# Two chained expert layers: another form of the first layer's division, and another order of its products

## The chip, the cores and the metric

The kernel runs on one core of a Trainium2 chip. The metric is the device time of one execution in microseconds; less is better. Three timed runs of the kernel before gave 1129.43, 1130.37 and 1132.01 us, with the median 1130.37 us.

## The reference, cut to what matters

6080 tokens of width 256 pass a gated scan over time and then two layers with 2048 hidden columns each. All of it is float32.

```python
h = f[:, t] * h + i[:, t] * x[:, t]            # the scan, f = lb + (1 - lb) * sigmoid(f_logit)

h = x @ w_in                                   # stage 1
P = a[0] + a[1] * h + a[2] * h**2 + a[3] * h**3
Q = 1.0 + np.abs(b[0]) * np.abs(h) + np.abs(b[1]) * h**2
g = P / (Q + 1e-06)
x2 = g @ w_out

h = x2 @ w_in                                  # stage 2, with weights of its own
r = np.maximum(h, 0.0)
out = (r * r) @ w_out
```

## The kernel before, in words

Tokens are cut into 12 blocks, the first of 448 tokens and eleven of 512 (`BLOCKS`). The 2048 hidden columns of a stage are taken 256 at a time, so a block has `NP` = 8 **steps** for each stage. From the third loop on (line 727), one step of stage 1, `a`, runs beside one step of stage 2, `b`, which lies `LAG` = 9 steps behind. "Position" below is a step's number in its block of stage 1, 0 to 7. A matrix product is made of a high and a low part of both operands: three terms, each a pass of matmuls with 512 tokens, as `mm1` and `mm2` show. So one full step of the third loop has 12 matmuls of `S1_mm1` (tile `h`), 12 of `S2_mm1` (tile `hb`), 12 of `S1_mm2` (tile `acc`, inputs `g1h` and `g1l`) and 12 of `S2_mm2` (inputs `g2h` and `g2l`), of which the last four, `S2_mm2_low`, are held over to the next step.

The order on each engine is the order in which the program is written (`manual_schedule`); every engine takes its own instructions strictly in that order. Blocks 0 and 1 go through two loops of their own (lines 658 and 691), where part of the work still is in single float32 products; the third loop begins with block 2.

In a step of the third loop, stage 1 runs as follows. `s1_scalar` (line 402) reads the products `h` from PSUM: ScalarE writes `u` = |h| (L412) and `s` = a3 h + a2 (L420), GpSimd writes `t` = |b1| u + |b0| (L414). `s1_quad` (L432) on VectorE makes `t` = t u, which is Q without its constant. `s1_poly` (L424, L425) makes `s` the polynomial without a0. `s1_rsqrt` (L446, L447) makes `u` about 1/Q on ScalarE, as the square of a reciprocal root. `s1_ratio` (L461, L464) makes `t` = Q u and `s` = -P u; the sign comes from `pna`, which line 565 has negated. `s1_high` (L470) rounds -s to the high part `g1h` on ScalarE. `s1_low` (L475, L478) corrects the quotient, (t - 2) s, and leaves the low part `g1l`, both on VectorE. `g1h` and `g1l` have one buffer each; `u`, `t`, `s` and `r` have two; the PSUM tile `h` has one, so the next `S1_mm1` can start only when `s1_poly` has read it.

Stage 2 is `s2_relu` (L485) and `s2_square` (L491, L496) on ScalarE, and `s2_low` (L501), which makes `g2l` on GpSimd one step later. Ahead of it stands a copy of one element of `t` on GpSimd (L751): it makes `g2l` wait until `s1_quad` of the same step is done.

`ahead` (line 603) puts the preparation of the next block into certain positions: loads of `z` at 2 and of `x` at 3, the gate `pre_gate` at 3 (two transposes on VectorE, a tanh with a table load on ScalarE, two operations on GpSimd), transposes `pre_in` at 4, a multiplication and a scan at 5 and 6. `split_x` (L319, L320) follows at 7, `out_store` at 2. At position 0 of the next block `to_x2` (L509, L510) turns the finished sum `acc` into `x2h` and `x2l`, the input of stage 2. `z`, `x` and the output tile share one buffer.

The order of the products is set by lines 764 and 777:

```python
            if ap is not None and (ends or a is None or not bp[0]):
                S1_mm2(*ap)
            ...
            if ap is not None and not (ends or a is None or not bp[0]):
                S1_mm2(*ap)
```

In a full step `S1_mm2` so comes behind `S2_mm2_high`; where a block ends (`ends`, position 0), ahead of it.

Of the kernel before, what the change touches and what calls it, by code (L numbers as in the profile page):

```python
# [15 lines left out]
P = 128  # L16
# [8 lines left out]
def hgru_two_moe_kernel(  # L25
# [49 lines left out]
    def f32(ap):  # L75
        return ap.bitcast(F32)
# [184 lines left out]

    def pre_gate(j):
        n = BLOCKS[j]
        t = pt.pop(("z", j))
        for dc in range(KD):
            sg = pre.tile([P, NMAX], F32, tag="sg", name="sg")
            nc.vector.transpose(sg[:, :n], squares(t, j)[:, :, dc::KD])
            nc.scalar.activation(out=sg[:, :n], in_=sg[:, :n], func=ACTF.Tanh, scale=0.5)
# [4 lines left out]
            pt["f", j, dc] = sg  # L273

# [174 lines left out]
    def s1_single(a, h, u, t, s):  # L449
# [4 lines left out]
        nc.vector.scalar_tensor_tensor(  # L454
            out=g, in0=t, scalar=2.0, in1=s, op0=ALU.subtract, op1=ALU.mult
        )
# [10 lines left out]

    def s1_high(a, s):
        fh = chain_tile("g1h", F32R, BLOCKS[a[0]])
        nc.scalar.activation(out=fh, in_=s, func=ACTF.Copy, scale=-1.0)  # L470
        return fh

    def s1_low(a, t, s, fh, eng):
        fl = chain_tile("g1l", F32R, BLOCKS[a[0]])
        nc.vector.scalar_tensor_tensor(  # L475
            out=t, in0=t, scalar=2.0, in1=s, op0=ALU.subtract, op1=ALU.mult
        )
        eng.tensor_tensor(out=fl, in0=t, in1=f32(fh), op=ALU.subtract)  # L478
        g1[a] = (fh, fl)
# [23 lines left out]

    def to_x2(j):
        n = BLOCKS[j]
        a = acc.pop((1, j))
        h = io.tile([P, KD, NMAX], F32R, tag="x2h", name="x2h")
        l = io.tile([P, KD, NMAX], F32R, tag="x2l", name="x2l")
        nc.scalar.activation(out=h[:, :, :n], in_=a[:, :, :n], func=ACTF.Copy)  # L509
        nc.vector.tensor_tensor(  # L510
# [31 lines left out]
    with tc.manual_schedule():  # L542
# [115 lines left out]
        for i in range(NP):  # L658
# [32 lines left out]
        for s in range(NP, 2 * NP):  # L691
# [35 lines left out]
        for s in range(2 * NP, n1 + LAG + 1):  # L727
# [8 lines left out]
            if a is not None:  # L736
# [32 lines left out]
            if bp is not None and not last_hand_over:  # L769
# [52 lines left out]
```

## Time and profile before

| what | us |
|---|---|
| median of three runs | 1130.37 |
| the profiled execution | 1131.16 |
| its span in the trace | 1129.2 |
| TensorE busy with matmuls | 1106.3 (98%) |
| VectorE busy | 984.2 (87%) |
| ScalarE busy | 886.9 (79%) |
| GpSimd busy | 439.5 (39%) |

The profiled execution's own time is 1131.16 us, 2.0 us above its span, and 0.8 us above the median. PE is TensorE's matmuls, PEld its weight loads, DVE is VectorE, ACT is ScalarE, POOL is GpSimd, SP issues most transfers. A row of the timeline has the start in the span, the length, the engine, the line and the tiles (out<-in), and in brackets how long the engine was idle before and who ended that. Two instructions of one engine overlap a little in such rows, so what an instruction costs its engine is read from start to start. A row of the windows view has the stretch, its length, and for each engine the busy time and in brackets the instructions. Matmul lengths in the rows are modelled; starts are what to go by.

### The profile page before, as it was taken

How to read it: one execution, taken by the hardware profiler on the slowest of the kernel's cores; microseconds unless marked ns; L12 is line 12 of the kernel's file. 1: busy time of each engine (PE TensorE's matmuls, PEld its weight loads, DVE VectorE, ACT ScalarE, POOL GpSimd, SP SyncE). 2: the span in 40 equal slices, each digit the busy share in tenths (PEclk: the TensorE clock that was granted, in tenths of full speed). 3: DMA queues.
4: the chain of work that ended last, by engine and by line, in shares of the span. 5: the costliest groups of instructions: out<-in, count | busy, mean ns of one | idle time of the engine just before them, and what ended most of it. 6: DMA issues, size and time to landing. Idle time of an engine off the chain costs nothing.

```text
span 1129.2 us, 12488 instructions
## 1 busy us (share of the span) xinstructions
PE 1106.3 (98%) x4594; PEld 860.4 (76%) x4594; DVE 984.2 (87%) x885; ACT 886.9 (79%) x993; POOL 439.5 (39%) x308
## 2 busy tenths in 40 slices
PE   8999999999999999999999999999999999999997
PEld 5446666777887887887888788788788788788876
DVE  6998998889989989989989989989998998998732
ACT  5866987987787887887787787788788788787754
POOL 3536542344343353444343343444334344433200
PEclk9999999999999999999999999999999999999999
DMA  9943322320200200110020030030021021010010
GB/s 248 338 124 70 73 45 49 73 37 1 38 19 1 38 20 1 19 38 1 5 53 1 1 57 1 1 57 1 1 38 19 1 38 19 0 20 1 1 19 19
DMA packets 107164, 44.65 MB, mean 40 GB/s; under 512 B 95840, under 2 KB 96736, under 8 KB 107104
## 3 DMA queue, kind: packets, MB, share of 16 engines
q1 hardware_dynamic: 103136, 35.21, 13.9%
q0 software_dynamic: 2448, 8.39, 4.0%
q8 instruction: 36, 0.59, 0.2%
q10 hardware_dynamic: 1520, 0.27, 0.1%
q14 instruction: 24, 0.20, 0.1%
HBM read 29.23 MB, written 6.23 MB: 31 GB/s over the span
## 4 chain that ended last, share of the span: by engine, by line
PE 43%; DVE 25%; issue 6%; ACT 3%; POOL 1%; DVEq 0%; ACTq 0%
PE acc L346 21%; PE hb L332 12%; PE h L332 11%; DVE s L424 4%; DVE s L425 4%; DVE s L464 3%; DVE t L432 3%; DVE g1l L478 3%; DVE t L461 2%; DVE t L475 2%; POOL t L414 1%; DVE sg L299 1%; DVE x1l L320 1%; ACT g1h L470 1%; DVE x2l L510 1%
## 5 line engine op out<-in xcount | busy, mean ns | idle before, releaser
L414 POOL TENSOR_SCALAR t<-u,pb 128x1024 f32<-128x1024 f32 x88 | 136.1, 1547 | 358.6 <-ACT u L412 358.6
L332 PE MATMUL hb<-x2h,wi 128*128 128x512 f32 (+1 forms) x768 | 203.9, 387 | 0.0
L501 POOL TENSOR_TENSOR g2l<-r,g2h 128x1024 fp32r<-128x1024 f32 x78 | 188.4, 2416 | 8.4 <-PE acc L346 8.2
L346 PE MATMUL acc<-g2h,wo 128*128 128x512 f32 x704 | 174.9, 390 | 1.1 <-ACT g2h L496 0.7
L332 PEld LDWEIGHTS hb<-x2h,wi 128*128 128x128 f32 x768 | 144.2, 188 | 29.0
L346 PEld LDWEIGHTS acc<-g2h,wo 128*128 128x128 f32 x704 | 132.2, 188 | 30.1 <-ACT g2h L496 2.0
L432 DVE TENSOR_TENSOR t<-t,u 128x1024 f32<-128x1024 f32 x88 | 107.0, 1216 | 50.3 <-POOL t L414 50.3
L485 ACT ACTIVATE r<-hb 128x512 f32<-128x512 f32 (+1 forms) x192 | 109.4, 593 | 50.8 <-PE hb L332 47.9
L446 ACT ACTIVATE u<-t 128x1024 f32<-128x1024 f32 x88 | 93.4, 1061 | 65.5 <-DVE t L432 65.1
L478 DVE TENSOR_TENSOR g1l<-t,g1h 128x1024 fp32r<-128x1024 f32 x80 | 126.2, 1578 | 18.0 <-ACT g1h L470 9.2
L461 DVE SCALAR_TENSOR_TENSOR t<-t,u 128x1024 f32<-128x1024 f32 x88 | 121.8, 1385 | 9.9 <-ACT u L447 7.9
L470 ACT ACTIVATE g1h<-s 128x1024 fp32r<-128x1024 f32 x80 | 84.8, 1060 | 52.7 <-DVE s L464 52.7
L425 DVE SCALAR_TENSOR_TENSOR s<-s,pna,h 128x1024 f32<-128x1024 f32 (+1 forms) x96 | 121.9, 1270 | 3.4
L464 DVE SCALAR_TENSOR_TENSOR s<-s,pna,u 128x1024 f32<-128x1024 f32 (+1 forms) x96 | 121.3, 1264 | 0.0
L332 PE MATMUL h<-x1h,wc 128*128 128x512 f32 x352 | 115.7, 410 | 5.3 <-DVE s L425 5.3
L332 PE MATMUL hb<-x2l,wi 128*128 128x512 f32 (+1 forms) x384 | 117.5, 387 | 0.0
L424 DVE TENSOR_TENSOR s<-s,h 128x1024 f32<-128x1024 f32 (+1 forms) x96 | 115.3, 1201 | 1.9 <-ACT u L412 1.6
L332 PE MATMUL h<-x1l,wc 128*128 128x512 f32 x352 | 109.6, 392 | 0.0
L332 PE MATMUL h<-x1h,wd 128*128 128x512 f32 x352 | 109.1, 391 | 0.0
L412 ACT ACTIVATE u<-h 128x1024 f32<-128x1024 f32 (+1 forms) x96 | 96.3, 1003 | 15.5 <-PE h L332 14.0
L420 ACT ACTIVATE s<-h,pna 128x1024 f32<-128x1024 f32 (+1 forms) x88 | 104.8, 1191 | 0.0
L496 ACT ACTIVATE g2h<-r 128x1024 fp32r<-128x1024 f32 x88 | 93.4, 1062 | 14.3 <-PE acc L346 4.5
(123 smaller groups left out, 1848.5 us busy)
## 6 DMA issues: line engine op xcount, KB each, us to landing
wi<-in_moe_w_in_dram SPq DMA_DIRECT2D x16, 512.0 KB, 7.6
wo<-in_moe_w_out_dram SPq DMA_DIRECT2D x16, 512.0 KB, 8.9
z<-in_f_logit_dram SPq DMA_DIRECT2D x44, 128.0 KB, 3.3
x<-in_x_dram SPq DMA_DIRECT2D x44, 128.0 KB, 3.2
out_dram<-o SPq DMA_DIRECT2D x84, 64.0 KB, 2.0
wd<-wa POOLq DMA_DIRECT2D x4, 512.0 KB, 4.9
wi<-wa POOLq DMA_DIRECT2D x4, 512.0 KB, 4.6
wo<-whole POOLq DMA_DIRECT2D x4, 512.0 KB, 4.8
```

The source lines that it names most:

```text
L332: nc.tensor.matmul(out=o, lhsT=ws[a][:, k, fs], rhs=xs[b][:, k, :n], start=(q == 0 and k == 0), stop=(q == len(terms) - 1 and k == KD - 1),)
L346: nc.tensor.matmul(out=acc[:, dc, :n], lhsT=ws[a][:, c, dc::KD] if spread else ws[a][:, c, dc * P:(dc + 1) * P], rhs=gs[b][:, c, :n], star ...
L414: nc.gpsimd.tensor_scalar(out=t, in0=u, scalar1=pb[:, 1:2], scalar2=pb[:, 0:1], op0=ALU.mult, op1=ALU.add)
L420: nc.scalar.activation(**linear)
L424: nc.vector.tensor_tensor(out=s, in0=s, in1=h, op=ALU.mult)
L425: nc.vector.scalar_tensor_tensor(out=s, in0=s, scalar=pna[:, 1:2], in1=h, op0=ALU.add, op1=ALU.mult)
L432: nc.vector.tensor_tensor(out=t, in0=t, in1=u, op=ALU.mult)
L461: nc.vector.scalar_tensor_tensor(out=o, in0=q, scalar=QC, in1=r, op0=ALU.add, op1=ALU.mult)
L464: nc.vector.scalar_tensor_tensor(out=s, in0=s, scalar=pna[:, 0:1], in1=u, op0=ALU.add, op1=ALU.mult)
L478: eng.tensor_tensor(out=fl, in0=t, in1=f32(fh), op=ALU.subtract)
L485: nc.scalar.activation(out=r[:, c, :], in_=h2.pop((*b, c))[:, :m], func=ACTF.Relu)
L501: eng.tensor_tensor(out=gl, in0=r, in1=f32(gh), op=ALU.subtract)
```

## The change

It does four things, all but the first from block 2 on or at its border.

1. `pna` is no longer negated. `s1_single` (blocks 0 and 1) subtracts the other way round instead.
2. The division is written anew. ScalarE makes `u` = |b0 h| and `t` = h squared from PSUM, then `s`. GpSimd's operation on `t` goes. VectorE makes `t` = |b1| t + u. After the reciprocal, `s1_divide` makes the high part as `g1h` = P u, rounded on VectorE as it is written, then the remainder P - Q g1h in two operations, and `g1l` = remainder times u. ScalarE's copy to `g1h` goes.
3. `S1_mm2` stands ahead of `S2_mm2_high` in all steps. `s2_relu` moves on ScalarE behind the reciprocal.
4. `to_x2` is cut in two, both ahead of the division: the high part behind `s2_relu`, the low part behind `s2_square`. `pre_gate` loses its transposes to `pre_turn`, which stands behind the polynomial of position 3; the rest of the gate stands ahead of the division.

```diff
@@ s1_scalar
+        if a[0] > 1:
+            nc.scalar.activation(out=u, in_=h, func=ACTF.Abs, scale=pb[:, 0:1])
+            nc.scalar.activation(out=t, in_=h, func=ACTF.Square)
+            nc.scalar.activation(**linear)
+            return h, u, t, s
@@ s1_quad
+        if a[0] > 1:
+            nc.vector.scalar_tensor_tensor(
+                out=t, in0=t, scalar=pb[:, 1:2], in1=u, op0=ALU.mult, op1=ALU.add
+            )
+            return [(t, u, t)]
@@ s1_high and s1_low give way to s1_divide
+    def s1_divide(a, h, u, t, s):
+        n = BLOCKS[a[0]]
+        fh = chain_tile("g1h", F32R, n)
+        fl = chain_tile("g1l", F32R, n)
         nc.vector.scalar_tensor_tensor(
-            out=t, in0=t, scalar=2.0, in1=s, op0=ALU.subtract, op1=ALU.mult
-        )
-        eng.tensor_tensor(out=fl, in0=t, in1=f32(fh), op=ALU.subtract)
+            out=fh, in0=s, scalar=pna[:, 0:1], in1=u, op0=ALU.add, op1=ALU.mult
+        )
+        nc.vector.scalar_tensor_tensor(
+            out=t, in0=t, scalar=QC, in1=f32(fh), op0=ALU.add, op1=ALU.mult
+        )
+        nc.vector.scalar_tensor_tensor(
+            out=t, in0=s, scalar=pna[:, 0:1], in1=t, op0=ALU.add, op1=ALU.subtract
+        )
+        nc.vector.tensor_tensor(out=fl, in0=t, in1=u, op=ALU.mult)
         g1[a] = (fh, fl)
@@ the third loop
                 if nj is not None and a[1] == NP - 1:
                     split_x(nj)
+                if nj is not None and a[1] == 3:
+                    pre_turn(nj)
...
             if b is not None:
                 S2_mm1(*b)
-                r = s2_relu(b)
-            if ap is not None and (ends or a is None or not bp[0]):
+            if ap is not None:
                 S1_mm2(*ap)
...
-            if ap is not None and not (ends or a is None or not bp[0]):
-                S1_mm2(*ap)
             if a is not None:
                 s1_rsqrt(q, *c)
-                s1_ratio(q, *c)
+            if b is not None:
+                r = s2_relu(b)
+            if ends:
+                to_x2_high(ap[0])
             if b is not None:
                 later = s2_square(b, r)
...
             do_splits(s)
+            if nj is not None and a[1] == 3:
+                pre_gate(nj)
+            if ends:
+                to_x2_low(ap[0])
+            if a is not None:
+                s1_divide(a, *c)
             ahead(a, ap)
-            if a is not None:
-                fh = s1_high(a, c[3])
-                s1_low(a, c[2], c[3], fh, nc.vector)
```

How instructions stand on VectorE, at position 0 of a middle block (tiles as above; the numbers behind `h` and `acc` are buffers). Before:

```order
L432 TENSOR_TENSOR t<-t,u 128x1024
L424 TENSOR_TENSOR s<-s,h_4456 128x1024
L425 SCALAR_TENSOR_TENSOR s<-s,pna,h_4456 128x1024
L461 SCALAR_TENSOR_TENSOR t<-t,u 128x1024
L464 SCALAR_TENSOR_TENSOR s<-s,pna,u 128x1024
L510 TENSOR_TENSOR x2l<-acc_3917,x2h 128x1024
L475 SCALAR_TENSOR_TENSOR t<-t,s 128x1024
L478 TENSOR_TENSOR g1l<-t,g1h 128x1024
```

And now:

```order
L443 SCALAR_TENSOR_TENSOR t<-t,pb,u 128x1024
L435 TENSOR_TENSOR s<-s,h_4415 128x1024
L436 SCALAR_TENSOR_TENSOR s<-s,pna,h_4415 128x1024
L535 TENSOR_TENSOR x2l<-acc_3872,x2h 128x1024
L489 SCALAR_TENSOR_TENSOR g1h<-s,pna,u 128x1024
L492 SCALAR_TENSOR_TENSOR t<-t,g1h 128x1024
L495 SCALAR_TENSOR_TENSOR t<-s,pna,t 128x1024
L498 TENSOR_TENSOR g1l<-t,u 128x1024
```

Seven operations of stage 1 stood in a step and seven stand there now; `x2l`, which stood inside the division, stands ahead of it.

On ScalarE, position 0, from the first reading of `h` to the end of the step. Before:

```order
L412 ACTIVATE u<-h_4456 128x1024
L420 ACTIVATE s<-h_4456,pna 128x1024
L485 ACTIVATE r<-hb 128x512 x2
L446 ACTIVATE u<-t 128x1024
L447 ACTIVATE u<-u 128x1024
L491 ACTIVATE r<-r 128x1024
L496 ACTIVATE g2h<-r 128x1024
L509 ACTIVATE x2h<-acc_3917 128x1024
L470 ACTIVATE g1h<-s 128x1024
```

And now:

```order
L419 ACTIVATE u<-h_4415,pb 128x1024
L420 ACTIVATE t<-h_4415 128x1024
L421 ACTIVATE s<-h_4415,pna 128x1024
L462 ACTIVATE u<-t 128x1024
L463 ACTIVATE u<-u 128x1024
L505 ACTIVATE r<-hb 128x512 x2
L527 ACTIVATE x2h<-acc_3872 128x1024
L511 ACTIVATE r<-r 128x1024
L516 ACTIVATE g2h<-r 128x1024
```

The copy to `g1h` at the end is gone, the square of `h` is new, and the two readings of `hb` stand behind the reciprocal.

On TensorE, a plain step (position 1; `acc_4592` and `acc_4539` are stage 1's sums, `acc_3999` and `acc_3973` stage 2's), behind the six rows of `h`. Before:

```order
L346 MATMUL acc_3999<-g2l,wo_1146 128x512 x4
L332 MATMUL hb<-x2l,wi_560 128x512 x2
L346 MATMUL acc_3999<-g2h,wo_1146 128x512 x8
L346 MATMUL acc_4592<-g1h,wa_1004 128x512 x4
L346 MATMUL acc_4592<-g1l,wa_1004 128x512 x4
```

And now:

```order
L351 MATMUL acc_3973<-g2l,wo_1145 128x512 x4
L337 MATMUL hb<-x2l,wi_559 128x512 x2
L351 MATMUL acc_4539<-g1h,wa_1003 128x512 x4
L351 MATMUL acc_4539<-g1l,wa_1003 128x512 x4
L351 MATMUL acc_3973<-g2h,wo_1145 128x512 x8
```

The eight matmuls on `g2h` changed places with the twelve on `g1h` and `g1l`; the row of `hb` stands for four, and rows with the other half of the weights are left out here.

## Rows read from the trace of the kernel before

**Rows 1.** The page, busy time of each engine over the span.
```profile
PE 1106.3 (98%) x4594; PEld 860.4 (76%) x4594; DVE 984.2 (87%) x885; ACT 886.9 (79%) x993; POOL 439.5 (39%) x308
```

**Rows 2.** Windows (stretch, length, PE, PEld, DVE, ACT, POOL): block 2, blocks 3 to 10, seven steps of block 11.
```profile
178.62:268.94 90.32, 88.99 (x370) 68.75 (x369) 78.52 (x71) 76.27 (x88) 36.13 (x27) 1.00 0.25 45
268.94:977.45 708.51, 704.41 (x3073) 573.55 (x3073) 652.39 (x569) 574.06 (x633) 286.83 (x209) 1.00 0.10 19
977.45:1054.45 77.00, 76.79 (x337) 62.92 (x337) 66.19 (x56) 60.38 (x66) 27.09 (x22) 1.00 0.05 8
```

**Rows 3.** Windows: single steps, from one start of `S1_mm1` to the next.
```profile
568.23:579.11 10.88, 10.88 (x49) 9.01 (x48) 8.81 (x8) 8.51 (x10) 3.76 (x3) 1.00 0.24 50
...
611.88:623.31 11.43, 11.15 (x50) 8.94 (x49) 11.19 (x11) 9.22 (x12) 4.71 (x4) 1.00 0.00 1
...
201.64:212.63 10.99, 10.62 (x47) 8.35 (x46) 9.84 (x10) 10.22 (x12) 4.75 (x4) 1.00 0.54 88
```

**Rows 4.** Waits in blocks 3 to 11: engine, line, releaser, us in total, times, longest.
```profile
PE h L332 <- DVE s L425: 4.6, 19, 0.3
...
DVE t L432 <- POOL t L414: 42.9, 29, 1.8
```

**Rows 5.** Timeline, DVE and POOL, steps at 534.74, 557.20, 568.23, 600.87.
```profile
544.35 2.42 POOL L501 TENSOR_TENSOR g2l<-r,g2h 128x1024 fp32r<-128x1024 f32 x1 [0.91 <-PE acc L346]
545.57 2.29 DVE L461 SCALAR_TENSOR_TENSOR t<-t,u 128x1024 f32<-128x1024 f32 x1
...
568.09 1.27 DVE L464 SCALAR_TENSOR_TENSOR s<-s,pna,u 128x1024 f32<-128x1024 f32 x1
569.40 1.22 DVE L475 SCALAR_TENSOR_TENSOR t<-t,s 128x1024 f32<-128x1024 f32 x1
570.76 1.23 DVE L478 TENSOR_TENSOR g1l<-t,g1h 128x1024 fp32r<-128x1024 f32 x1
573.52 1.23 DVE L432 TENSOR_TENSOR t<-t,u 128x1024 f32<-128x1024 f32 x1 [1.54 <-POOL t L414]
...
602.68 0.68 DVE L286 SCALAR_TENSOR_TENSOR bx<-sg,bx 128x512 f32<-128x512 f32 x1
604.79 1.22 DVE L475 SCALAR_TENSOR_TENSOR t<-t,s 128x1024 f32<-128x1024 f32 x1
604.93 2.15 POOL L414 TENSOR_SCALAR t<-u,pb 128x1024 f32<-128x1024 f32 x1 [4.45 <-ACT u L412]
606.14 2.01 DVE L478 TENSOR_TENSOR g1l<-t,g1h 128x1024 fp32r<-128x1024 f32 x1
608.07 1.21 DVE L432 TENSOR_TENSOR t<-t,u 128x1024 f32<-128x1024 f32 x1
609.21 1.21 DVE L424 TENSOR_TENSOR s<-s,h 128x1024 f32<-128x1024 f32 x1
609.49 2.41 POOL L501 TENSOR_TENSOR g2l<-r,g2h 128x1024 fp32r<-128x1024 f32 x1
610.45 1.28 DVE L425 SCALAR_TENSOR_TENSOR s<-s,pna,h 128x1024 f32<-128x1024 f32 x1
```

**Rows 6.** Timeline: ScalarE, the step at 568.23.
```profile
571.15 1.03 ACT L412 ACTIVATE u<-h 128x1024 f32<-128x1024 f32 x1 [0.63 <-PE h L332]
```

**Rows 7.** Groups of ACT instructions by line and shape: busy us, mean ns.
```profile
L420 ACT ACTIVATE s<-h,pna 128x1024 f32<-128x1024 f32 x80 | 96.0, 1200 | 0.0
...
L446 ACT ACTIVATE u<-t 128x1024 f32<-128x1024 f32 x88 | 93.4, 1061 | 65.5 <-DVE t L432 65.1
...
L412 ACT ACTIVATE u<-h 128x1024 f32<-128x1024 f32 x88 | 89.0, 1011 | 11.6 <-PE h L332 11.6
...
L268 ACT ACT_TABLE_LOAD x11 | 14.1, 1283 | 0.2
```

**Rows 8.** Timeline of SP: the loads of `z` in the same step.
```profile
568.82 1.92 SPq L217 DMA_DIRECT2D z<-in_f_logit_dram  x4
```

**Rows 9.** The page, DMA issues: kilobytes each, microseconds to landing.
```profile
z<-in_f_logit_dram SPq DMA_DIRECT2D x44, 128.0 KB, 3.3
```

More of the change, by code (lines that the diff above doesn't have):

```diff
@@ L260, in first_mul, with pre_turn @@
             pt["b", 0, dc] = bx
-    def pre_gate(j):
+    def pre_turn(j):
         n = BLOCKS[j]
@@ L267, in pre_gate @@
             nc.vector.transpose(sg[:, :n], squares(t, j)[:, :, dc::KD])
+            pt["f", j, dc] = sg
+    def pre_gate(j):
+        n = BLOCKS[j]
+        for dc in range(KD):
+            sg = pt["f", j, dc]
             nc.scalar.activation(out=sg[:, :n], in_=sg[:, :n], func=ACTF.Tanh, scale=0.5)
@@ L272, in pre_gate @@
             )
-            pt["f", j, dc] = sg
     def pre_in(j):
@@ L454, in s1_single @@
         nc.vector.scalar_tensor_tensor(
-            out=g, in0=t, scalar=2.0, in1=s, op0=ALU.subtract, op1=ALU.mult
+            out=g, in0=t, scalar=2.0, in1=s, op0=ALU.subtract, op1=ALU.mult, reverse0=True
         )
@@ L466, in s1_ratio @@
         )
[L468 to L474, printed above, removed]
+    def s1_divide(a, h, u, t, s):
+        n = BLOCKS[a[0]]
+        fh = chain_tile("g1h", F32R, n)
+        fl = chain_tile("g1l", F32R, n)
         nc.vector.scalar_tensor_tensor(
-            out=t, in0=t, scalar=2.0, in1=s, op0=ALU.subtract, op1=ALU.mult
+            out=fh, in0=s, scalar=pna[:, 0:1], in1=u, op0=ALU.add, op1=ALU.mult
         )
-        eng.tensor_tensor(out=fl, in0=t, in1=f32(fh), op=ALU.subtract)
+        nc.vector.scalar_tensor_tensor(
[5 more added lines that the diff above has]
+        nc.vector.tensor_tensor(out=fl, in0=t, in1=u, op=ALU.mult)
         g1[a] = (fh, fl)
@@ L502, in s2_low, with to_x2_high, to_x2_low @@
         g2[b] = (gh, gl)
-    def to_x2(j):
+    def to_x2_high(j):
+        n = BLOCKS[j]
+        h = io.tile([P, KD, NMAX], F32R, tag="x2h", name="x2h")
+        nc.scalar.activation(out=h[:, :, :n], in_=acc[1, j][:, :, :n], func=ACTF.Copy)
+        x2[j] = (h,)
+    def to_x2_low(j):
         n = BLOCKS[j]
         a = acc.pop((1, j))
-        h = io.tile([P, KD, NMAX], F32R, tag="x2h", name="x2h")
+        (h,) = x2[j]
         l = io.tile([P, KD, NMAX], F32R, tag="x2l", name="x2l")
-        nc.scalar.activation(out=h[:, :, :n], in_=a[:, :, :n], func=ACTF.Copy)
         nc.vector.tensor_tensor(
@@ L564, in hgru_two_moe_kernel @@
         nc.vector.tensor_scalar(out=be, in0=lbt, scalar1=0.5, scalar2=0.5, op0=ALU.mult, op1=ALU.add)
-        nc.vector.tensor_scalar(out=pna, in0=pna, scalar1=-1.0, scalar2=None, op0=ALU.mult)
         def warm(by, of, times):
@@ L609, in ahead @@
                 if a[1] == 3:
-                    pre_gate(nj)
-                if a[1] == 3:
                     pre_load("x", xf, nj)
@@ L617, in ahead @@
                     pre_scan(nj, a[1] - 5)
-            if ap is not None and ap[0] and ap[1] == NP - 1:
-                to_x2(ap[0])
         def finish_single(a, q, c):
@@ L674, in hgru_two_moe_kernel @@
             if i == 2:
+                pre_turn(1)
                 pre_gate(1)
@@ L713, in hgru_two_moe_kernel @@
                 S1_mm1(1, 1)
-                to_x2(0)
+                to_x2_high(0)
+                to_x2_low(0)
             if i:
@@ L721, in hgru_two_moe_kernel @@
             do_convert(scale, s + 1)
+            if i == 3:
+                pre_turn(2)
+                pre_gate(2)
             ahead(a, ap)
```

## The prediction

> **What bounds the kernel now.** I read the page first: TensorE is busy 98% of the span, VectorE 87%, and nothing else comes near [rows 1]. So the question is what TensorE still waits for, and where. The windows view, cut at the starts of `S1_mm1`, answers that. A full step has 48 matmuls, and the step at 568.23 takes 10.88 us with PE busy in all of it [rows 3]: 10.88 / 48 = 0.227 us for each matmul, and no wait. That is the floor that this change cannot go below, since it leaves every matmul in place. Positions 5 to 7 and 0 to 2 are longer; the step at 611.88 takes 11.43 [rows 3]. Over blocks 3 to 10, 64 steps take 708.51 us [rows 2], against 64 x 10.88 = 696.32.
>
> The waits view names the cause: `S1_mm1` waits for L425, the last reading of the one PSUM tile `h` [rows 4]. The timeline shows how near that is [rows 5]: in the step at 600.87 VectorE starts the quadratic (L432) at 608.07, 7.20 us into the step, and L425 ends at 610.45 + 1.28 = 611.73, 3.66 us after that; the next step starts 0.15 later, at 611.88 [rows 3]. So TensorE waits whenever L432 starts later than 10.88 - 3.66 - 0.15 = **7.07 us** into its step. Where VectorE is not late, L432 starts at 573.52 - 568.23 = 5.29, then held by GpSimd's `t` [rows 4, 5]. Two things make it late: extra work (602.68 to 604.79 is 2.11 us for multiplication and scan [rows 5]), and a collision: L478 takes 2.01 us where GpSimd's L414 runs across it, and 1.23 alone [rows 5].
>
> **What the waits are worth.** Blocks 3 to 10: 708.51 - 696.32 = 12.19. Seven steps of block 11: 77.00 - 76.16 = 0.84 [rows 2]. Block 2: its last five steps, 212.63 to 268.94, take 56.31 against 54.40, so 1.91 [rows 2, 3]; its third, with 44 matmuls, takes 10.99 against 44 x 0.227 = 9.97 [rows 3], of which I take 0.65, since a change of operand type at its start is part of the rest. Its first two steps still have single-precision products and are left as they are. Together **15.6 us** is all that there is to win.
>
> **The change, part by part.**
>
> *GpSimd's `t` goes, ScalarE makes it.* Readings of `h` begin 571.15 - 568.23 = 2.92 us into a step [rows 6]. `u` with one scale per partition lies between 1.01 (none) and 1.20 (two) [rows 7]; I take 1.10. The square reads the same tile, 1.01. The quadratic then starts at about 2.92 + 1.10 + 1.01 = 5.0, against 5.29. The 2.15 us of GpSimd that held VectorE up no longer exist. ScalarE loses one pass of 1.0 (`g1h`) and gains one: its load of 574.06 / 8 = 71.8 us a block [rows 2] stays far below 87.04.
>
> *VectorE's step.* Seven operations stay seven. From start to start, a new form costs what its nearest row does: quadratic 1.14 (608.07 to 609.21), polynomial 1.24 (609.21 to 610.45) and 1.31, then the four operations of the division, each reading the one before, 1.31, 1.36, 1.31 (568.09 to 569.40 to 570.76) and 1.14: **8.8 us**, of which the division is 5.1 and starts 3.7 after the quadratic [rows 5]. With the scan it is 10.9. Over a block VectorE was busy 652.39 / 8 = 81.5 us with the collisions in it [rows 2]; the same work is at most that now, against 87.04 of TensorE.
>
> *How late VectorE gets.* A plain step starts its quadratic at 5.0. Position 3 adds a table load of 1.28 [rows 7] and two tanh to ScalarE's end, behind `g2h`, which must wait for `S2_mm2_high` to leave its one buffer at the step's end; `u` of position 4 so begins some 0.6 late, and a second table load now stands straight ahead of the reciprocal. I reckon that the quadratic starts at 5.6 at positions 4 and 5, 5.7 at 6 and 7. At position 0 the new order makes a wait: `x2h` stands behind reciprocal, square and `s2_relu`, so `x2l` ends some 6.7 after the quadratic's start (1.25 + 1.06 + 1.06 + 1.1 + 1.0 + 1.2 by the rows nearest [rows 5, 7]) and the division behind it 5.1 later. VectorE stands idle 1.8 us there, and position 1 starts at about 5.9. All of these are below 7.07, by 1.2 or more, so I set the waits of plain blocks to nothing.
>
> *The order of TensorE.* `g1h` has one buffer, so the division's first write must wait for the eight matmuls on the old one. Ahead of `S2_mm2_high` these are the 29th to 36th of the step and done at about 36 x 0.227 + 0.2 = 8.4; the division starts at 5.0 + 3.7 = 8.7. In the old place they were done at 10.2, and VectorE would have waited 1.5 us in each step: the cover is 0.3, and with it gone the division slips by what is missing. In return the products wait for a division that ends at 13.8, 2.9 into the next step; they use its low part 8.2 into it.
>
> *Queues moved past.* The transposes of `z` now start 5.0 + 3.7 = 8.7 into position 3. The four loads leave SP by 570.74 and take 3.3 to land [rows 8, 9], 5.8 into the step: 2.9 to spare. The loads of `x` follow the transposes and so come earlier. The negation of four columns at the head, the tail (where `x2h` now goes ahead of one square) and blocks 0 and 1 I cost at nothing, with 1 us either way.
>
> *Left over.* In block 2 ScalarE also splits weights, two passes in each of five steps; at positions 3 and 4 they meet the table loads, and the quadratic gets to about 7.0. I leave 0.6 us of waits for block 2 and the start of block 3. **Sum: 15.6 - 0.6 = 15.0.** The profiled execution took 1131.16, so 1116.2 by its own time; it lies 0.8 above the median of three, and against that median, 1130.37, the forecast is **1115.4 us**. The scatter of the runs shown is 0.2%, so a difference over 0.2% (2.3 us) is what a measurement can tell from none.
>
> **Rivals.**
>
> *Half the waits stay (1122.6).* GpSimd's gate operations now fall on the end of position 3's division and on the quadratic of position 4. The nearest GpSimd row with one input took 2.15 against a colliding VectorE [rows 5]; two such on top of 5.6 pass 7.07. With 0.4 us of waiting at position 4 and again at position 1, 18 times, 7.2 us of the gain are lost. For it: the margin is 1.2. Against: GpSimd has nothing else left in that stretch, so that the pair can be done before the quadratic of position 4.
>
> *No change (1130.4).* The change would not do what it says if the quadratic still started at 7.2: VectorE's step would have to be 0.7 longer than reckoned. An unseen form that writes a rounded result could do it. Against: L478 writes the same type in 1.23 [rows 5].
>
> *Slower, `g2l` under the division (1157).* All four operations of the division read two SBUF tiles. L461, of that kind, lasted 2.29 us where `g2l` was under way: it finished 1.09 after `g2l`'s end at 546.77 [rows 5]. L424 and L425, with one input in PSUM, keep 1.21 and 1.28 beside it. Today `g2l` starts 609.49 - 608.07 = 1.42 after the quadratic and ends at 3.83 [rows 5], so 0.13 of it lies over a division that starts at 3.7. Each microsecond that it starts later would cost VectorE one. The spare is (87.04 - 81.5 - 1.8) / 8 = 0.47 a step; the kernel before stands 0.19 above the floor; so from 0.66 us on it is slower than before, and at 1 us 0.34 x 79 steps = 27 us. Against it: the copy that releases `g2l` still follows the quadratic directly.
> [...]
>
> *VectorE as the bound (1079).* If matmuls could be packed more tightly, a block would take VectorE's 81.5 + 1.8 = 83.3 us and 3.7 x 9.9 blocks = 37 us more would go. The rows speak against it: 48 matmuls without any wait take 10.88 [rows 3].
> [...]
>
> **How the numbers follow.** Forecast 0.76, half the waits 0.13, no change 0.05, slower 0.05, VectorE as the bound 0.01. The forecast's own range is 1113 (all 15.6 and the fastest of the runs shown, 1129.43, with a little at the tail) to 1118. The range given, 1113 to 1123, takes in the half case. Faster: 0.76 + 0.13 + 0.01 = 0.90; same 0.05; slower 0.05.
>
> **What would show it.** Right: steps of 10.88 at positions 5 to 7 and 0 to 2; blocks 3 to 10 at 697; the quadratic at 5.0 to 5.9 into its step; no wait of `S1_mm1` for the polynomial; `g1l`'s operation at 1.2 us. Wrong: a wait of `S1_mm1` or `S1_mm2` for VectorE in each step, operations of the division at 2 us beside `g2l`, or a division that waits for TensorE to leave `g1h`.

## The result, and the profile after

The changed kernel takes **1115.46 us** in the median of four runs (1115.11 to 1117.15); the kernel before, beside it, 1130.53 (1129.43 to 1132.01). The ratio is 0.9871, with an interval of 0.9856 to 0.9886. The forecast was 1115.4. The profiled execution took 1115.11 us, with a span of 1113.20.

The page, busy time of each engine, which answers to [rows 1], and the chain that ended last, followed back from the last instruction:

```profile
PE 1095.6 (98%) x4594; PEld 863.1 (78%) x4594; DVE 965.5 (87%) x884; ACT 891.7 (80%) x993; POOL 309.8 (28%) x228
...
PE 93%; ACT 2%; DVE 2%; DMA 1%; issue 1%; DVEq 0%; ACTq 0%
```

The chain on the page of before:

```profile
PE 43%; DVE 25%; issue 6%; ACT 3%; POOL 1%; DVEq 0%; ACTq 0%
```

TensorE's and VectorE's shares of busy time do not differ from before, 98% and 87% in both; they could not have told this result. The chain can: TensorE now is 93% of it, and was 43%, with 25% for VectorE.

Windows of the kernel after, for the stretches of [rows 2]: block 2, blocks 3 to 10, seven steps of block 11. The fourth row is the tail.

```profile
177.20:265.44 88.24, 88.21 (x371) 69.03 (x369) 78.68 (x71) 77.36 (x88) 21.33 (x19) 1.00 0.25 46
265.44:962.11 696.67, 696.67 (x3072) 576.86 (x3073) 634.71 (x570) 578.43 (x635) 181.52 (x145) 1.00 0.10 19
962.11:1038.27 76.16, 76.16 (x337) 63.09 (x336) 65.52 (x56) 60.24 (x65) 17.94 (x14) 1.00 0.05 8
1038.27:1113.20 74.93, 67.86 (x293) 54.96 (x291) 27.88 (x27) 39.92 (x47) 2.55 (x2) 0.97 0.08 15
```

Length and PE busy are the same number in blocks 3 to 11: TensorE shows no idle time there. Against [rows 2], block 2 is 90.32 - 88.24 = 2.08 shorter, blocks 3 to 10 708.51 - 696.67 = 11.84, block 11 0.84: **14.8 us**. The spans differ by 1129.23 - 1113.20 = 16.03. Of the rest, 1.38 is the first product of the span, which starts at 13.46 and not 14.84; in the other traces of this study it starts anywhere from 13.4 to 15.5, so I put this down to the execution and not the change. Blocks 0 and 1 differ by 0.04, and the tail, 74.78 before, is 0.15 longer.

Single steps of the kernel after (positions 4, 0 and 1), which answer to [rows 3]:

```profile
570.43:581.31 10.88, 10.88 (x49) 9.01 (x48) 8.20 (x8) 10.51 (x12) 4.76 (x4) 1.00 0.21 48
613.95:624.83 10.88, 10.88 (x49) 9.01 (x48) 9.15 (x8) 9.05 (x10) 1.68 (x2) 1.00 0.01 2
624.83:635.71 10.88, 10.88 (x49) 9.01 (x48) 10.32 (x9) 8.39 (x10) 3.46 (x3) 1.00 0.00 0
```

The waits of blocks 3 to 11 (in order: total, times, longest), which answer to [rows 4]:

```profile
...
ACT u L419 <- PE h L337: 52.6, 63, 1.6
...
DVE t L443 <- ACT t L420: 24.6, 20, 1.7
...
DVE x2l L535 <- ACT x2h L527: 14.9, 9, 1.7
```

`S1_mm1` no longer waits for the polynomial. What is left are waits of the other engines, for TensorE and for each other. The wait of 42.9 us for GpSimd's `t` [rows 4] has become one of 24.6 for ScalarE's.

The timeline of VectorE and GpSimd in the steps at 613.95 and 624.83 (positions 0 and 1; the division of the second runs on into the next step), to be read against [rows 5]:

```profile
619.65 1.28 DVE L443 SCALAR_TENSOR_TENSOR t<-t,pb,u 128x1024 f32<-128x1024 f32 x1
...
623.33 2.40 POOL L521 TENSOR_TENSOR g2l<-r,g2h 128x1024 fp32r<-128x1024 f32 x1 [2.08 <-PE acc L351]
625.04 1.23 DVE L535 TENSOR_TENSOR x2l<-acc,x2h 128x1024 fp32r<-128x1024 f32 x1 [1.66 <-ACT x2h L527]
626.18 1.28 DVE L489 SCALAR_TENSOR_TENSOR g1h<-s,pna,u 128x1024 fp32r<-128x1024 f32 x1
...
631.29 1.28 DVE L443 SCALAR_TENSOR_TENSOR t<-t,pb,u 128x1024 f32<-128x1024 f32 x1
632.49 1.21 DVE L435 TENSOR_TENSOR s<-s,h 128x1024 f32<-128x1024 f32 x1
632.84 2.42 POOL L521 TENSOR_TENSOR g2l<-r,g2h 128x1024 fp32r<-128x1024 f32 x1
633.74 1.28 DVE L436 SCALAR_TENSOR_TENSOR s<-s,pna,h 128x1024 f32<-128x1024 f32 x1
635.15 1.28 DVE L489 SCALAR_TENSOR_TENSOR g1h<-s,pna,u 128x1024 fp32r<-128x1024 f32 x1
636.55 1.23 DVE L492 SCALAR_TENSOR_TENSOR t<-t,g1h 128x1024 f32<-128x1024 f32 x1
637.81 1.28 DVE L495 SCALAR_TENSOR_TENSOR t<-s,pna,t 128x1024 f32<-128x1024 f32 x1
639.20 1.23 DVE L498 TENSOR_TENSOR g1l<-t,u 128x1024 fp32r<-128x1024 f32 x1
```

In a plain step `g2l` starts 632.84 - 631.29 = 1.55 after the quadratic and ends at 635.26, 0.11 into the first operation of the division, which still takes 1.28. At position 0 `g2l` comes late, at 623.33, held by TensorE; what lies beside it there is VectorE's idle time and `x2l`, which reads PSUM and takes 1.23 (1224 ns on average), and the division starts at 626.18, behind `g2l`'s end. The experiments show what that is worth.

ScalarE and GpSimd at position 4 (the step at 570.43), the place of the first rival:

```profile
571.79 1.28 ACT L274 ACT_TABLE_LOAD   x1
573.09 1.16 ACT L274 ACTIVATE sg<-sg 128x512 f32<-128x512 f32 x2
573.83 2.21 POOL L275 TENSOR_SCALAR sg<-sg,al,be 128x512 f32<-128x512 f32 x2 [5.31 <-ACT sg L274]
574.15 1.10 ACT L419 ACTIVATE u<-h,pb 128x1024 f32<-128x1024 f32 x1
575.14 1.01 ACT L420 ACTIVATE t<-h 128x1024 f32<-128x1024 f32 x1
576.19 1.28 DVE L443 SCALAR_TENSOR_TENSOR t<-t,pb,u 128x1024 f32<-128x1024 f32 x1 [1.56 <-ACT t L420]
```

The gate on GpSimd ends at 573.83 + 2.21 = 576.04, and the quadratic starts at 576.19, released by ScalarE. It takes its usual 1.28, and the last operation of position 3's division, at 573.41, its usual 1.23 beside the start of the gate.

### The profile page after: what moved, and what is told of

It reads as the page before. It is cut to its first block, busy times and chain, and to the rows that moved or that the text cites. A ratio compares the mean times of both kernels' runs of the same rounds, so it can differ in the third digit from the quotient of the medians.

```text
span 1113.2 us, 12472 instructions
## 1 busy us (share of the span) xinstructions
PE 1095.6 (98%) x4594; PEld 863.1 (78%) x4594; DVE 965.5 (87%) x884; ACT 891.7 (80%) x993; POOL 309.8 (28%) x228
## 3 DMA queue, kind: packets, MB, share of 16 engines
q1 hardware_dynamic: 103136, 35.21, 13.6%
## 4 chain that ended last, share of the span: by engine, by line
PE 93%; ACT 2%; DVE 2%; DMA 1%; issue 1%; DVEq 0%; ACTq 0%
PE acc L351 46%; PE hb L337 23%; PE h L337 22%; PE q L454 2%; DMA wo<-in_moe_w_out_dram 1%; DMA z<-in_f_logit_dram 0%; ACT u L423 0%; DVE s L435 0%; ACT g2h L516 0%; DVE wa L182 0%; DVE t L477 0%; ACT u L462 0%; DVE sg L304 0%; ACT wo L167 0%; DVE s L480 0%
## 5 line engine op out<-in xcount | busy, mean ns | idle before, releaser
L778 POOL COPY turn<-t 128x1 f32<-128x1 f32 x78 | 14.3, 184 | 546.1 <-DVE t L443 546.1
L419 ACT ACTIVATE u<-h,pb 128x1024 f32<-128x1024 f32 x80 | 89.3, 1116 | 58.8 <-PE h L337 58.8
L443 DVE SCALAR_TENSOR_TENSOR t<-t,pb,u 128x1024 f32<-128x1024 f32 x80 | 101.8, 1272 | 30.9 <-ACT t L420 30.9
L505 ACT ACTIVATE r<-hb 128x512 f32<-128x512 f32 (+1 forms) x192 | 102.6, 582 | 18.8 <-PE hb L337 18.8
L489 DVE SCALAR_TENSOR_TENSOR g1h<-s,pna,u 128x1024 fp32r<-128x1024 f32 x80 | 102.4, 1280 | 13.3 <-ACT u L463 7.5
L337 PE MATMUL h<-x1h,wc 128*128 128x512 f32 x352 | 113.0, 402 | 0.0
L492 DVE SCALAR_TENSOR_TENSOR t<-t,g1h 128x1024 f32<-128x1024 f32 x80 | 98.1, 1226 | 9.1 <-DVE g1h L489 0.5
L495 DVE SCALAR_TENSOR_TENSOR t<-s,pna,t 128x1024 f32<-128x1024 f32 x80 | 102.8, 1285 | 2.8
L498 DVE TENSOR_TENSOR g1l<-t,u 128x1024 fp32r<-128x1024 f32 x80 | 98.0, 1225 | 7.7
L463 ACT ACTIVATE u<-u 128x1024 f32<-128x1024 f32 (+1 forms) x96 | 101.2, 1054 | 3.0
```

Of the source, the lines that this page charges most:

```text
L337: nc.tensor.matmul(out=o, lhsT=ws[a][:, k, fs], rhs=xs[b][:, k, :n], start=(q == 0 and k == 0), stop=(q == len(terms) - 1 and k == KD - 1),)
L443: nc.vector.scalar_tensor_tensor(out=t, in0=t, scalar=pb[:, 1:2], in1=u, op0=ALU.mult, op1=ALU.add)
L463: nc.scalar.activation(out=u, in_=u, func=ACTF.Square)
L489: nc.vector.scalar_tensor_tensor(out=fh, in0=s, scalar=pna[:, 0:1], in1=u, op0=ALU.add, op1=ALU.mult)
L492: nc.vector.scalar_tensor_tensor(out=t, in0=t, scalar=QC, in1=f32(fh), op0=ALU.add, op1=ALU.mult)
L495: nc.vector.scalar_tensor_tensor(out=t, in0=s, scalar=pna[:, 0:1], in1=t, op0=ALU.add, op1=ALU.subtract)
```

## The experiments

All were run beside the kernel before, which took 1129.13 to 1130.12 in them; "Q alone" is the kernel before with nothing but ScalarE's Q. Medians follow.

### Which part pays: the order alone, and Q alone

`e1_order_alone` is the kernel before with one condition gone:

```diff
-            if ap is not None and (ends or a is None or not bp[0]):
+            if ap is not None:
                 S1_mm2(*ap)
```

and the second `S1_mm2` left out. 

> The kernel before with S1_mm2 always ahead of S2_mm2_high, nothing else. My theory (VectorE is late because of GpSimd's t and its collisions; the order only frees g1h earlier for a division that VectorE writes): the old division does not wait for g1h, so nothing is won: 1130 us, 1128 to 1133. Rival (the order of the products itself is what pays): 1122 or less.

1135.34, ratio 1.0051 (1.0036 to 1.0066): slower than either theory said. A middle block takes 89.1 us for 88.56 before, and position 6, 11.01 before, takes 11.4.

`e5_q_alone` is the kernel before with the two hunks of the diff in `s1_scalar` and `s1_quad`. 

> The kernel before with Q from ScalarE's |b0 h| and square from block 2 on, GpSimd's t gone; old division, order and places. ScalarE has one more pass of 1.0 us a step, 80 us a block against 87. My theory: without the collisions VectorE's step is 9.0 and the quadratic stays below 7.07 into the step nearly everywhere: 1116 to 1119 us. Rival (the division from the remainder, which takes ScalarE's g1h out of the chain, is needed for the gain): 1124 or more.

1116.55, ratio 0.9884 (0.9868 to 0.99). 13.6 us under the kernel before of its set, of the change's 15. Its blocks 3 to 10 stand at the floor, as with the whole change:

```profile
267.49:964.00 696.51, 696.51 (x3073) 576.34 (x3072) 637.40 (x570) 630.52 (x697) 189.07 (x144) 1.00 0.11 19
```

`e4_t_from_gpsimd` is the change without these two hunks:

```diff
-        if a[0] > 1:
-            nc.scalar.activation(out=u, in_=h, func=ACTF.Abs, scale=pb[:, 0:1])
-            nc.scalar.activation(out=t, in_=h, func=ACTF.Square)
...
-            nc.vector.scalar_tensor_tensor(
-                out=t, in0=t, scalar=pb[:, 1:2], in1=u, op0=ALU.mult, op1=ALU.add
-            )
...
```

> The changed kernel, but |h| on ScalarE and t = b1 u + b0 on GpSimd as before; new division, order and places kept. My theory: the quadratic starts at about 5.3 in plain steps, and where VectorE runs into GpSimd's t (the scan of positions 5 and 6) each pays for the other, so part of the waits comes back: 1118 to 1124 us. Rival (the new division is what pays): 1115 to 1117. Second rival (GpSimd's operation is all of it): 1128 or more.

1143.07, ratio 1.012 (1.0103 to 1.0137): a miss, and slower than before. The groups of VectorE in that run (busy us, mean ns) show where:

```profile
L437 DVE TENSOR_TENSOR t<-t,u 128x1024 f32<-128x1024 f32 x88 | 106.8, 1214 | 42.4 <-POOL t L419 42.4
...
L304 DVE TENSOR_TENSOR_SCAN sg<-sg,carry,bx 128x512 f32<-128x512 f32 x22 | 41.7, 1893 | 0.8
```

The scan takes 1893 ns on average and 1284 in the change: GpSimd's `t` lies across it, and at other places across the end of the division, where `g1l` takes 1334 ns on average and 1225 in the change. Positions 1 and 7 take 12.2 and 11.84 us; the quadratic starts 8.4 and 8.0 us into them, past the 7.07 of the prediction. So GpSimd's `t` cost in two ways, as a wait of the quadratic (42.4 over the whole span here, 50.3 on the page of before) and as a collision, and the other parts alone do not avoid either. No run takes the two apart.

### The division, the order and the places

`e2_old_order` is the change with the products in the old order:

```diff
-            if ap is not None:
+            if ap is not None and (ends or a is None or not bp[0]):
                 S1_mm2(*ap)
...
+            if ap is not None and not (ends or a is None or not bp[0]):
+                S1_mm2(*ap)
```

> The changed kernel with the old order of products (S2_mm2_high ahead of S1_mm2 where no block ends). My theory: g1h is left by TensorE at 10.2 instead of 8.4 into the step, so the division starts 1.3 to 1.5 later in each plain step, VectorE idles there, and the quadratic of the steps behind a scan starts at about 6.7, still below 7.07: 1115 to 1119 us, with a wait of g1h for PE in the trace of over 60 us in total. Rival (the order is needed for the gain): 1123 or more.

1119.23, ratio 0.9904 (0.9889 to 0.9919): in the range, 3.8 above the change. But the wait that should have made it is small. The waits view has `g1h` wait 9.4 us for TensorE, 14.7 for ScalarE's `r` and 2.4 for nothing named, 0.3 a step together. The division does not read `r`; the timeline shows what ends such a wait, here at position 4:

```profile
580.38 1.98 PE L351 MATMUL acc<-g1h,wa 128*128 128x512 f32 x8
582.45 1.28 DVE L489 SCALAR_TENSOR_TENSOR g1h<-s,pna,u 128x1024 fp32r<-128x1024 f32 x1 [1.06 <-ACT r L505]
```

The eight matmuls on the old `g1h` end at 582.36, and the division starts 0.09 later, 10.23 us into its step, the 10.2 of the prediction. So all three read as waits for TensorE, of 0.30 to 1.06 us at positions 2 to 5; at the others the division comes later than 10.2 by itself. The steps at positions 0 and 2 are the long ones, 11.1. Their quadratics start at 6.3 and 6.2, so it is not the polynomial that holds them; what does is not worked out here.

`e6_old_division` is the change with the old division in the new one's place:

```diff
+        s1_ratio([(t, u, t)], h, u, t, s)
+        nc.scalar.activation(out=fh, in_=s, func=ACTF.Copy)
         nc.vector.scalar_tensor_tensor(
-            out=fh, in0=s, scalar=pna[:, 0:1], in1=u, op0=ALU.add, op1=ALU.mult
+            out=t, in0=t, scalar=2.0, in1=s, op0=ALU.subtract, op1=ALU.mult, reverse0=True
         )
...
-        nc.vector.tensor_tensor(out=fl, in0=t, in1=u, op=ALU.mult)
+        nc.vector.tensor_tensor(out=fl, in0=t, in1=f32(fh), op=ALU.subtract)
```

> The changed kernel with the old division (product, correction, ScalarE's copy to g1h, difference) at the place of the new one; Q, order and places as changed. My theory: seven operations of VectorE as before and no collision, the copy finds ScalarE free at the end of a step: 1115 to 1118 us. Rival (the division from the remainder pays): 1122 or more.

1125.26, ratio 0.9962 (0.9947 to 0.9977): a miss. The timeline of this run behind position 3 shows the longest wait of the chain that I had left out:

```profile
576.95 1.06 ACT L512 ACTIVATE g2h<-r 128x1024 fp32r<-128x1024 f32 x1 [0.63 <-PE acc L351]
578.03 1.28 ACT L274 ACT_TABLE_LOAD   x1
579.33 1.15 ACT L274 ACTIVATE sg<-sg 128x512 f32<-128x512 f32 x2
580.39 1.05 ACT L490 ACTIVATE g1h<-s 128x1024 fp32r<-128x1024 f32 x1
581.47 1.22 DVE L494 TENSOR_TENSOR g1l<-t,g1h 128x1024 fp32r<-128x1024 f32 x1 [2.18 <-ACT g1h L490]
```

`g2h` waits for TensorE to leave its buffer; the table load and the tanh stand behind it, then the copy to `g1h`, and VectorE, which has been done with its own part, waits 2.18 us for that copy. In the middle blocks TensorE does not feel this wait, since the steps behind it take 10.88; they lose at positions 0 to 2 (11.10, 11.27 and 11.00). At the border of positions 0 and 1 the queue holds the other way round:

```profile
635.70 1.06 ACT L490 ACTIVATE g1h<-s 128x1024 fp32r<-128x1024 f32 x1 [1.53 <-DVE s L480]
...
638.71 1.28 DVE L443 SCALAR_TENSOR_TENSOR t<-t,pb,u 128x1024 f32<-128x1024 f32 x1 [0.46 <-ACT t L420]
```

The copy waits 1.53 us for VectorE's `s`, the readings of the next `h` stand behind the copy, and the quadratic, which waits for them, starts 7.38 us into its step. Another 3.2 us lie in block 2 (91.48 for 88.24), where positions 4 and 5 take 13.08 and 12.08 and ScalarE splits weights besides. The old division takes VectorE through ScalarE's queue in every step; the new one does not.

Order and places were both new in that run, so two more kernels took them apart. `e9_q_and_order` is Q alone plus the edit of the first experiment. 

> The kernel before with Q from ScalarE and S1_mm2 always ahead of S2_mm2_high; the old division in its old places. It asks why the old division lost 8.7 us against the change when it stood in the new place. Theory (the order costs it): the old division ends late, by way of ScalarE's copy, so products that come 8 matmuls earlier wait for it; then this run loses several microseconds against Q alone (1116.5): 1120 to 1126, and the steps of positions 0 to 2 are 11.0 to 11.3. Rival (the place costs it, behind x2 and the gate): 1116 to 1118, all steps of blocks 3 to 10 at 10.88.

`e10_old_division_old_order` is `e6_old_division` with the old order. 

> The change with the old division and the old order of the products, so that only the places of s2_relu, x2 and the gate are new beside Q. Theory (the order costs the old division): 1116 to 1119. Rival (the place costs it): 1122 to 1126, with positions 0 to 2 at 11.0 to 11.3 as with the new order.

1122.08 (0.993, 0.9916 to 0.9943) and 1121.03 (0.9921, 0.9907 to 0.9934). Neither theory holds alone: against Q alone (1116.49 in this set) the order costs 5.6, the places 4.5, and both together 8.7 (the runs of the first set). Blocks 2 to 11 alone, in the traces, give 5.2, 5.6 and 9.3. With the new order the long step of a middle block is position 5 (11.33), behind two waits of `g2h` for TensorE, of about 1 us each, which sum to 20.0 us in this run and are not among the waits of Q alone; positions 0 to 2, where I expected it, keep within 0.06 of 10.88, but for one step of 11.09. With the new places it is positions 1 and 2 (11.04 and 11.02) and again 2 us in block 2 (91.53 for 89.44). In the median over the blocks the quadratic starts at 7.45 at position 5 of the first run and at 7.17 at position 1 of the second, past 7.07 both times; why position 2 is long is open.

### What the other three parts add to Q

`e11_q_alone_again` and `e12_change_again` are Q alone and the whole change, on one chip. 

> Q from ScalarE alone once more, beside the whole change on one chip. If the other three parts bring something, it is the 1.26 us of block 2 that the two traces differ by: 1116.5, 1.0 to 1.5 above the change. Rival: the difference lies in single executions only, and both are within 0.5 us.

> The whole change once more, beside Q from ScalarE alone. Theory: 1115.4, 1.0 to 1.5 below it. Rival: within 0.5 us of it.

1116.49 (1116.18 to 1117.69) and 1114.73 (1113.83 to 1117.02): 1.76 apart, 0.16%, with ranges that overlap. By the medians alone that is below what I said a measurement can tell. The two spans differ by 3.8, and 2.59 of that lies ahead of block 2, which begins at 178.63 and 176.04; in the first trace of the change it begins at 177.20, so much of this is scatter between executions. The windows of block 2 and its positions 4 and 5 place it, Q alone first:

```profile
178.63:268.06 89.43, 88.47 (x370) 68.99 (x369) 77.52 (x71) 83.40 (x96) 21.18 (x19) 1.00 0.25 46
222.94:234.45 11.51, 11.04 (x50) 8.86 (x48) 8.89 (x9) 11.37 (x15) 4.88 (x5) 1.00 0.41 70
234.45:246.07 11.62, 11.13 (x49) 8.93 (x49) 9.58 (x9) 11.48 (x15) 3.42 (x4) 1.00 0.13 23
```

and the change:

```profile
176.04:264.22 88.18, 88.18 (x370) 68.99 (x369) 78.61 (x71) 77.26 (x88) 21.30 (x19) 1.00 0.25 47
220.31:231.19 10.88, 10.88 (x50) 9.01 (x49) 8.19 (x7) 10.70 (x13) 5.14 (x5) 1.00 0.35 72
231.19:242.07 10.88, 10.88 (x50) 9.01 (x49) 10.00 (x10) 10.27 (x14) 3.44 (x3) 1.00 0.14 24
```

ScalarE is the busiest of the helpers there, 11.4 us in a step of 11.5: it splits weights besides. Without the copy to `g1h`, eight passes fewer in the block, it keeps up, and the 1.25 us go. The first pair of traces shows the same (89.50 and 88.24). It is the new division and not the order or the places: with the new division and the old order block 2 takes 88.22, with Q and the new order 89.60, with Q and the new places 91.53. So the new division is worth 1.25 us in block 2, and nearly all other steps of both kernels stand at the floor.

### The price of `g2l` under the division

`e7_late_g2l` is the change with `g2l` released by the polynomial instead of the quadratic, so that it falls on the division:

```diff
-                    nc.gpsimd.tensor_copy(turn, c[2][:, 0, 0:1])
+                    nc.gpsimd.tensor_copy(turn, c[3][:, 0, 0:1])
```

> The changed kernel with g2l on GpSimd released by the polynomial (s) instead of the quadratic (t), so that it runs beside the division, whose four operations read two SBUF tiles each. The rival of the prediction on the slower side, by the lock: VectorE loses up to 2.4 us a step, a step takes about 12.4 us instead of 10.88: 1220 to 1250 us, with operations of the division at 2 us and more. If the two do not shut each other out: 1115 to 1118.

1219.74, ratio 1.0796 (1.0779 to 1.0812): the rival's outcome, 0.3 us under its range. What that text calls the lock is the price it took from the row of 2.29 us [rows 5]. A middle block takes 97.9 us. Its timeline, and the group of the division's second operation, which takes 1226 ns on average in the change:

```profile
627.33 2.40 POOL L521 TENSOR_TENSOR g2l<-r,g2h 128x1024 fp32r<-128x1024 f32 x1
627.60 3.22 DVE L489 SCALAR_TENSOR_TENSOR g1h<-s,pna,u 128x1024 fp32r<-128x1024 f32 x1 [0.54 <-ACT u L463]
```

```profile
L492 DVE SCALAR_TENSOR_TENSOR t<-t,g1h 128x1024 f32<-128x1024 f32 x80 | 183.0, 2287 | 2.8
```

The operation at 627.60 ends at 630.82, 1.09 after `g2l`'s end at 629.73, and is 3.22 - 1.28 = 1.94 longer than alone.
It lay beside `g2l` for 629.73 - 627.60 = 2.13 us, so nearly all of the overlap was lost. The row of 2.29 us [rows 5] agrees: there too VectorE's operation ended 1.09 after `g2l`.
Not all of the 104 us above the change is VectorE's: TensorE itself waits for the late `g2l`, 17.8 us between 265 and 1040.

`e3_x2_behind` moves `x2h` and `x2l` behind the division:

```diff
-            if ends:
-                to_x2_high(ap[0])
...
-            if ends:
-                to_x2_low(ap[0])
             if a is not None:
                 s1_divide(a, *c)
             ahead(a, ap)
+            if ends:
+                to_x2_high(ap[0])
+                to_x2_low(ap[0])
```

> The changed kernel with both parts of x2 behind the division and the next block's preparation. My theory: VectorE's idle time of 1.7 us at position 0 goes, but x2l is ready only about 5.1 into position 1, where S2_mm1 reads it at 4.5: some 0.6 us of TensorE's wait in each of ten blocks, 1119 to 1122 us. Rival (x2's place does not matter, as VectorE idles for it anyway): 1115 to 1116.

1148.34, ratio 1.0164 (1.0147 to 1.0182): a miss by 26 us. All of it lies at position 1, which takes 13.65 or 15.28 us. The timeline of VectorE, GpSimd and TensorE around 370, and two windows just behind the wait of position 1 (in the first the granted clock, third number from the end, fell, in the second not):

```profile
366.91 2.41 POOL L521 TENSOR_TENSOR g2l<-r,g2h 128x1024 fp32r<-128x1024 f32 x1 [2.09 <-PE acc L351]
367.08 3.31 DVE L489 SCALAR_TENSOR_TENSOR g1h<-s,pna,u 128x1024 fp32r<-128x1024 f32 x1
...
374.30 1.22 DVE L535 TENSOR_TENSOR x2l<-acc,x2h 128x1024 fp32r<-128x1024 f32 x1
375.57 0.73 PE L337 MATMUL hb<-x2l,wi 128*128 128x512 f32 x2 [2.47 <-DVE x2l L535]
```

```profile
376.00:380.00 4.00, 4.00 (x12) 3.11 (x11) 3.12 (x3) 3.20 (x5) 2.53 (x2) 0.57 0.01 4
286.00:292.20 6.20, 6.20 (x28) 5.12 (x28) 5.62 (x5) 4.16 (x5) 2.55 (x2) 1.00 0.01 3
```

Two things that I had not reckoned with. Without `x2l` in between, the division meets the late `g2l` of position 0 and loses 2.03 us beside it (3.31 for 1.28, its end 1.07 after that of `g2l`); and with four operations ahead of it `x2l` then comes so late that `S2_mm1` waits 2.47 us. In five of the nine blocks the step with that wait takes 15.28; the windows show the granted clock in two of these, 0.89 over the step (0.57 in the 4.00 us above), and in one of the other four, 1.00. The parts add up: 9 x (13.65 - 10.88) + 5 x (15.28 - 13.65) = 33.1, against 1148.34 - 1115.46 = 32.9 measured.

### How much room VectorE has

`e8_one_more` adds one VectorE operation of 512 columns behind each division:

```diff
                 s1_divide(a, *c)
+                nc.vector.tensor_tensor(out=c[1][:, 0, :], in0=c[1][:, 0, :], in1=c[1][:, 1, :], op=ALU.add)
```

> The changed kernel with one more VectorE operation of 512 columns (about 0.65 us from start to start) behind each division; it adds up the halves of u, which nobody reads any more. It measures the spare of VectorE. If the spare is what the busy time leaves (87.04 - 79.2 = 7.8 us a block against 5.2 added): 1115 to 1117 us. My theory: start to start VectorE's block takes 82.8 and stands idle 1.7 for x2h, so 2.6 are left and 5.2 cost 2.6 a block: 1130 to 1142 us.

1147.61, ratio 1.0155 (1.0139 to 1.0172). The 80 operations took 0.74 us each (59.1 us in all); about 32 of these show, 1147.61 - 1115.46. The theory's direction was right and its size too small. So VectorE's true spare is (59.1 - 32.2) / 80 = 0.34 us a step, though in the change it is busy 87% of the span. The waits of its quadratic show where the spare lay, in the change and then in this run:

```profile
L443 DVE SCALAR_TENSOR_TENSOR t<-t,pb,u 128x1024 f32<-128x1024 f32 x80 | 101.8, 1272 | 30.9 <-ACT t L420 30.9
L443 DVE SCALAR_TENSOR_TENSOR t<-t,pb,u 128x1024 f32<-128x1024 f32 x80 | 102.4, 1280 | 4.8 <-ACT t L420 4.8
```

The wait for ScalarE's `t` took up 26 of the 27 us. The wait for `x2h` at position 0, 1.66 a block, stays as it was, and positions 6, 7 and 1 became 11.7, 11.9 and 12.1.

## Why the prediction was right, point by point

**The floor and the waits** were right: 64 steps take 696.67, forecast 696.3. Of 15.6 us of waits 14.8 went, forecast 15.0. Some 0.7 are left where the prediction left 0.6: in block 2 and the first step of block 3. The third step of block 2, of which 0.65 was taken by estimate, went from 10.99 to 10.34, but with the order alone it does so too. What the estimate left out of the 1.02 stands at the step's start, where the operand type changes: the first two matmuls behind the single float32 products take 202.45 - 201.64 = 0.81 us, and 201.10 - 200.29 = 0.81 in the change, where the pairs that follow take 0.45 or 0.46. The rest of the difference of the medians lies within their scatter: that the forecast of 1115.4 was met to 0.1 us is luck, with four runs 2 us apart and 1.38 us from the start of the span. One reading was wrong and cost nothing: position 5 is not among the long steps of before (589.99 to 600.87 is 10.88).

**What makes the quadratic late** was right: GpSimd's `t` was the cause, and Q alone gives 13.6 us. The waits view had put only 4.6 of the 13 us of blocks 3 to 11 down to the polynomial [rows 4]; the starts tell more. In the median over the blocks, with Q alone, the quadratic starts at 5.96, 6.70, 6.39 and 6.28 at positions 0, 1, 6 and 7, where before it started at 7.23, 7.53, 7.20 and 7.61: the four were past 7.07, and none is now. `u` costs 1.10 and `t` 1.01, as taken.

**VectorE's step was mis-sized**, 9.05 us where 8.8 were reckoned: from the quadratic at 631.29 to the operation behind `g1l`, at 640.34. The first operation of the division starts 635.15 - 633.74 = 1.41 after the polynomial where I took 1.31, and 636.55 - 635.15 = 1.40, 1.26, 1.39 follow where I took 1.31, 1.36, 1.31. So the quadratic starts later than the 5.0 to 5.9 forecast: 5.70 into the step at position 0 (619.65 - 613.95), 6.46 at position 1 (631.29 - 624.83), 5.76 at position 4 (576.19 - 570.43), 6.10 and 6.38 at positions 6 and 7 (598.29 - 592.19, 609.45 - 603.07). The polynomial too ends later behind it, 633.74 + 1.28 - 631.29 = 3.73 for 3.66, so the limit was 7.0, and the margin 0.5 and not 1.2. It held, but 0.73 us more in each step, in the last experiment, did not fit: the spare was 0.34 a step and not the 0.47 that busy time gave.

**Position 0's detour** was right: VectorE waits 1.66 for `x2h`, forecast 1.8.

**The order of TensorE** was half right. That it pays with the new division is so (3.8 us), and the old `g1h` is left at 10.2 in the old place, as reckoned. The price of 1.5 us of VectorE's waiting in each step was too high; the waits are 0.3 a step, at four of the eight positions. And the prediction said nothing of what the order costs with the old division, 5 us: `g2h` leaves its buffer later, and what stands behind it on ScalarE with it. The four parts are not four gains. Order and places each cost 4 to 6 us with the old division; with the new one, which does not wait for ScalarE, the two together cost nothing. The new division in the old places was not run.

**The first rival** (the gate on GpSimd) did not come: it ended 0.15 us ahead of the quadratic, which is close. **The slower one** did not come either, with an overlap of 0.11 us where 0.13 was forecast; with `g2l` moved under the division, the kernel takes 104 us more. That the change does not do what it says, and VectorE as the bound, are out by the steps of 10.88.

What stays open is why the step with `x2l`'s wait takes 15.28 us in five blocks, with a granted clock of 0.89 where the windows show it, and 13.65 in the other four, after the same wait of 2.47 us.

## What to carry to other kernels

Cut the trace at the start of a repeated step, take the shortest one as the floor, and count what the others are above it: that sum (15.6 us here) told the gain to within a microsecond, where shares of busy time told nothing. Look for the engine whose queue a chain passes through without need: an operation moved from GpSimd to ScalarE paid 13.6 us by ending a wait and a collision at once, and a copy that took VectorE's division through ScalarE's queue turned edits that are free without it into losses of 4 to 6 us. Before moving an operation, see what it hides: `x2l` ahead of the division looked like a detour of 1.7 us and was the cover over GpSimd's `g2l`, beside which the division lost 2.03 us.

## What the runs showed of the hardware

In the changed kernel, blocks 3 to 11, what stands behind an operation of VectorE with 1024 columns starts 1.14 to 1.21 us after it where it does not read its result (630.15 to 631.29, 631.29 to 632.49), 1.24 to 1.27 where it reads that result (632.49 to 633.74, 636.55 to 637.81), and mostly 1.38 to 1.42 where the one ahead, besides, takes its scalar from a tile (635.15 to 636.55, 637.81 to 639.20). The last figure is no rule: the pair of 637.81 and 639.20 stands 1.32 apart at position 0 (628.83 to 630.15), and before, L475 starts 1.31 after L464, which is of that kind too (568.09 to 569.40 [rows 5]). Over the seven operations of a step the sum was 0.24 us more than reckoned.

In the run with `x2` behind the division, TensorE's granted clock, 1.00 in the windows ahead of it, was 0.57 over 4.00 us that TensorE was busy in from end to end (376.00 to 380.00), right behind a wait of 2.47 us. Over that whole step it was 0.89, and 0.89 over another of the long ones (459.83 to 475.12); in a step of 13.65 (278.60 to 292.25) the same wait left it at 1.00. A long step took 1.63 us more than a short one, two thirds as much again as the wait itself.
